# v loaded and cast to bf16 by GpSimd's own DMA queue instead of SyncE's loads and ScalarE's cast

## The chip, the core and the metric

The kernel runs on one core of one Trainium2 chip. The metric is device time in microseconds for one execution. Engines are called PE (TensorE), DVE (VectorE), ACT (ScalarE), POOL (GpSimd) and SP (SyncE, which issues DMAs). PEld is PE's weight load.

## The reference

Attention over 8 batches of 8 heads (576 rows, 64 columns a head) that keeps only the 32 largest scores of each row, and behind it two matmuls with a PReLU between them.

```python
def _attn_ref(q, k, v):
    scores = scale * np.matmul(q, k.transpose(0, 1, 3, 2))
    kth = np.partition(scores, -top_k, axis=-1)[..., -top_k:-top_k + 1]
    mask = scores >= kth
    scores = np.where(mask, scores, -1000000000.0)
    ...                                   # softmax over the kept scores
    return np.matmul(attn, v).astype(np.float32)

def _moe_ref(x, w_in, w_out, alpha):
    h = x @ w_in
    g = np.maximum(h, 0.0) + alpha * np.minimum(h, 0.0)
    return (g @ w_out).astype(np.float32)
```

The heads' outputs side by side are x, of 4608 rows and 512 columns; w_in goes to 2048 columns and w_out back to 512. All inputs and the output are float32.

## The kernel before, in words

The 64 heads are taken as 32 pairs. A pair has nine row blocks: eight of 128 rows (four per head) and a ninth that holds the last 64 rows of both heads. So there are 288 row blocks. The main loop counts ticks n, one per row block, and in each tick it writes instructions for several blocks at different stages. The order that is written is the order in which each engine's queue runs (a manual schedule). Steps that belong to a pair rather than to a row block are put into a calendar by `put(tick, eng, f)` and written by `run(tick, eng)`; "end" is the last place of a tick.

What happens to one row block, with the lines of the profile:

- PE computes scores into `ps` (L328). ACT adds a bias from `NT` (a guess at the limit of the row, made per pair from q and k) and writes `b` (L337), takes signs with a sum (`h`, L343), and the exponential `e` of two blocks at once (L348).
- POOL turns the sum of signs into a sign word `SG` (L353).
- DVE flips the scores by it (`y`, L359), takes the eight largest of six segments (`C`, L369), merges them (`L`, L384 and L386), picks one as the limit (L397 to L413), and seven blocks later compares `b` with the limit: `mk` (L433).
- POOL multiplies `mk` with `e` into the weights `w` (L443; for the ninth block `wm`, L443 and L449). SP issues the transposes of `w` into `wT` (L456, L451). PE multiplies `wT` with `v_bf` into `pu` (L494), DVE takes the reciprocal of the row sums (`rz`), and ACT scales the result into `xb` (L523).

Behind that run the two matmuls of the second part (`ph` L697, `gT` L703, `pz` L715), fed in between. Their weights are loaded in the first ticks; `w_in` comes through POOL's own DMA queue, eight loads with a cast to bf16 (L632).

In a tick, POOL's queue holds the product `w` of a block seven ticks back and then `SG` of the last block; DVE's queue holds `mk`, then the searches, then `y`. `w` needs `mk` of the same tick, and `y` needs `SG` of the same tick.

v is handled per pair. `v_bf` (six buffers) has ten column groups of 65: five of the first head, five of the second; group 4 holds only rows 0 to 63 and group 5 only rows 64 to 127, the other halves are zero. The 65th column is one, so that the matmul also gives row sums. `load_v(p)` (L147 to L154) issues four loads on SP into a float32 staging tile `st_v` (two buffers): 128 partitions x 4 rows, 64 rows, 64 rows and 128 x 4 rows, every row of 64 float32 values. `act_v` (L203) casts all of it to `v_bf` on ACT, a step of the pair's plan:

```python
ts = [-14, -13, -12, -11, -10, -9, -7, -6, -5, -5, -4, -4, -3, -2, -8]
...
dict(dve=[dve_6]), dict(act=[act_v])]
```

The last entry of `ts` places the cast eight ticks ahead of `BASE[p]`, which for the first pairs is the tick of the pair's first block (9 p). Pairs 12 and on have their plans 9 to 18 ticks earlier. The loads of `load_v` are written 13 ticks ahead of `BASE[p]`. For pair 0 the cast comes in tick -2, ahead of the first bias pass.

Of the kernel before, what the change touches and what calls it, by code (L numbers as in the profile page):

```python
# [9 lines left out]
FP32 = mybir.dt.float32  # L10
# [6 lines left out]
S = 576  # L17
# [15 lines left out]
def kernel(  # L33
# [10 lines left out]
    nc = tc.nc  # L44
    B, H, S_, D = q.shape
# [5 lines left out]
    NPAIR = (B * H) // 2  # L51
# [7 lines left out]
    V1 = D + 1  # L59
# [31 lines left out]
    vf = v.rearrange("b h s d -> (b h) s d")  # L91

    main = ExitStack()
    prep = main.enter_context(tc.tile_pool(name="prep", bufs=2))
# [13 lines left out]
    M8 = prep.tile([128, NT], FP32, name="M8", bufs=1)  # L108
    GKs = [prep.tile([128, 130], BF16, name=f"GK{i}", bufs=1) for i in range(2)]
    ksts = [prep.tile([128, 5, 130], FP32, name=f"kst{i}", bufs=1) for i in range(2)]  # L110
    st_vs = [prep.tile([128, 10, D], FP32, name=f"st_v{i}", bufs=1) for i in range(2)]
    NV = 6
    v_bfs = [prep.tile([128, 10, V1], BF16, name=f"v_bf{i}", bufs=1) for i in range(NV)]
    NQ = 5
# [2 lines left out]
    def early_sets():  # L117
        for i in range(2):
            nc.gpsimd.memset(ksts[i][:, :, 0:1], 1.0)
            nc.gpsimd.memset(ksts[i][:, :, 129:130], 1.0)  # L120
            nc.gpsimd.memset(ksts[i][64:128, 4, :], 0.0)
        for t_ in st_vs:
            nc.vector.memset(t_[64:128, 4, :], 0.0)
            nc.vector.memset(t_[0:64, 5, :], 0.0)
        for t_ in v_bfs:
            nc.vector.memset(t_[:, :, D:V1], 1.0)
            nc.vector.memset(t_[64:128, 4, D:V1], 0.0)
            nc.vector.memset(t_[0:64, 5, D:V1], 0.0)
        for i in range(KW):
            nc.vector.memset(iota[:, i:i + 1], (1.0 + 2 * i) ** 2)  # L130

    pairs = {}

    def load(p, eng2=None):
        hA = 2 * p
        st_q = prep.tile([128, 5, 128], FP32, name="st_q")
        st_k = ksts[p % 2]
        for src, st, o, en in ((qf, st_q, 0, nc.sync), (kf, st_k, 1, eng2 or nc.sync)):
            for side in range(2):
                en.dma_start(  # L140
                    st[:, 0:4, o + 64 * side:o + 64 * side + 64],
                    src[hA + side, 0:512, :].rearrange("(c p) d -> p c d", p=128))
            en.dma_start(st[0:64, 4, o:o + 128].rearrange("p (h d) -> p h d", h=2),
                         src[hA:hA + 2, 512:S, :].rearrange("h p d -> p h d"))
        pairs[p] = dict(q=st_q, k=st_k, st_v=st_vs[p % 2], v=v_bfs[p % NV])

    def load_v(p):  # L147
        hA = 2 * p
        st_v = st_vs[p % 2]
        nc.sync.dma_start(st_v[:, 0:4, :], vf[hA, 0:512, :].rearrange("(c p) d -> p c d", p=128))  # L150
        nc.sync.dma_start(st_v[0:64, 4, :], vf[hA, 512:S, :])
        nc.sync.dma_start(st_v[64:128, 5, :], vf[hA + 1, 0:64, :])
        nc.sync.dma_start(st_v[:, 6:10, :],
                          vf[hA + 1, 64:S, :].rearrange("(c p) d -> p c d", p=128))  # L154

    ORDER = [divmod(n, TPP) for n in range(N0)]
    LAST = range(P0, NPAIR)
# [5 lines left out]
    n = 0  # L163
# [7 lines left out]
    BASE = {p: TPP * (p - (p > LEAD1) - (p > LEAD2)) for p in range(NPAIR)}  # L171
# [3 lines left out]
    def prep_plan(p):  # L175
        d = pairs[p]
# [21 lines left out]

        def act_q():
            nc.scalar.copy(d["qkT"][:, 0, 0:512], d["pq"])  # L200

        def act_v():
            nc.scalar.copy(d["v"][:, :, 0:D], d["st_v"])  # L203

        def pe_k():
            d["pk"] = bank("pk", [128, 512])
# [82 lines left out]
                                    ALU.bitwise_xor, ALU.bitwise_or)  # L289

        if p == 1:
            ts = [-9, -8, -7, -6, -5, -4, -3, -2, -2, -2, -2, -2, -1, -1, 1]
        else:
            ts = [-14, -13, -12, -11, -10, -9, -7, -6, -5, -5, -4, -4, -3, -2, -8]
        dvx = "dve" if p < 2 else "dvx"
        steps = [dict(pe=[pe_q]), dict(act=[act_q], pe=[pe_k]), dict(act=[act_k], pe=[pe_t]),
                 dict(act=[act_t], pe=[pe_g]), dict(act=[act_g], pe=[pe_r]),
                 dict(dve=[dve_p]), dict(pe=[pe_s]), dict(act=[act_m]), dict(dve=[dve_2]),
                 {dvx: [dve_3]}, dict(dve=[dve_4]), {dvx: [dve_4b]}, dict(dve=[dve_5]),
                 dict(dve=[dve_6]), dict(act=[act_v])]  # L300
        if p == 0:
            ts = [-16, -15, -14, -13, -12] + [-11] * 6 + [-2]
            steps = [dict(pe=[pe_q, pe_g, pe_t]), dict(act=[act_q, act_g, act_t], pe=[pe_r, pe_k]),
                     dict(dve=[dve_p]), dict(act=[act_k], pe=[pe_s]), dict(act=[act_m])] + steps[8:]
        return list(zip(ts, steps))
# [35 lines left out]
    def act_s(n):  # L341
        h = attn.tile([128, S], BF16, name="h", bufs=1)
        nc.scalar.activation(h, tiles[n]["b"], AF.Sign, accum_out=S_all[:, n:n + 1])  # L343
# [406 lines left out]
    with tc.manual_schedule(engines={E.PE, E.Activation, E.DVE, E.Pool, E.SP}):  # L750
        cal = {}

        def put(tick, eng, f):
            cal.setdefault((tick, eng), []).append(f)

        def run(tick, eng):
            for f in cal.pop((tick, eng), ()):
                f()

        def plan(p):  # L760
            for dt, st in prep_plan(p):
                for eng, fs in st.items():
                    for f in fs:
                        put(BASE[p] + dt, eng, f)
# [55 lines left out]
        plan(0)  # L820
        plan(1)
        early_sets()
        load_v(0)
        load_v(1)
        for t in range(-16, 0):
            for eng in ("act", "pool", "pe", "dve"):
                run(t, eng)
# [7 lines left out]
        n = 0  # L835
        end = max(NT + 24, 0)
        while n < end or back or after:
            for p in range(2, NPAIR):
                if n == max(0, BASE[p] - 18):
                    load(p)  # L840
                    plan(p)
                if n == max(0, BASE[p] - 13):
                    load_v(p)
            banks[0] = 2 if n >= NT else 1 if n >= N0 + 2 else 0
            if n + 1 < NT and unit_of[n + 1][2] == 0:
                scores(n + 1)
            while after:
                after.popleft()()
            if n < NT:
                n0, m, i = unit_of[n]  # L850
                if i == 0:
                    act_b(n0)
                    if m == 2:
                        run(n, "act")
                    act_s(n)
                    if m == 1:
                        run(n, "act")
                        act_e(n0)
                else:
                    act_s(n)  # L860
                    run(n, "act")
                    act_e(n0)
            run(n, "act")
            if n >= 3 and n % 3 == 0 and n - 3 < NT:
                sel_a((n - 3) // 3)
            nb = 1 if n < N0 + 2 else 2
            credit = min(credit, 0.0) + (2.4 if n >= NT else 1.9)
            first = True
            while back and credit > 0.0 and (first or nb == 2):
                pe_f, act_f, cost, takes = back[0]  # L870
                if takes and len(after) >= nb:
                    break
                back.popleft()
                pe_f()
                if act_f:
                    after.append(act_f)
                credit -= cost
                first = False
            run(n, "pe")
            if n >= NT:  # L880
                run(n, "dve")
                run(n, "dvx")
            due = wdue.get(n, ())
            for wn in due:
                if wn < NW:
                    mask(wn)
            for f in held:
                f()
            held = []
            for wn in due:  # L890
                weights(wn, wn >= NW)
                tail_of(n, wn)
            if 0 <= n - 1 < NT:
                side_of(n - 1)
            segs = seg_ops(n - LAG_S) if 0 <= n - LAG_S < NT else []
            mn = n - LAG_M
            merges = merge_ops(mn) if 0 <= mn < NT else []
            pick = bool(merges) and mn % 3 == 2
            if pick and n >= NT:
                sel_eq(mn // 3)  # L900
            lm = n - LAG_M - 3
            for i in range(max(len(segs), len(merges), 2)):
                if i < len(segs):
                    segs[i]()
                if i < len(merges):
                    merges[i]()
            run(n, "dve")
            if 0 <= lm < NT and lm % 3 == 0:
                limit(lm // 3)
            if pick and n < NT:  # L910
                sel_eq(mn // 3)
            if 0 <= n - 1 < NT:
                flip(n - 1)
            run(n, "dvx")
            if pick:
                sel_pr(mn // 3)
                held = [lambda m=mn // 3: sel_sum(m)]
                if mn % TPP == TPP - 1:
                    put(n + 2, "dve" if mn < NT - 1 else "end", lambda g=mn // TPP: check_group(g))
                    if mn == NT - 1:  # L920
                        put(n + 2, "end", checks)
                        put(n + 3, "end", final_flag)
                        put(n + 7, "end", read_flag)
            run(n, "end")
            n += 1
# [139 lines left out]
```

## Time and profile before

| | |
|---|---|
| median of three runs | 873.0 us (871.04 to 874.72) |
| profiled execution | 873.98 us |
| its span | 872.1 us |
| DVE busy | 835.1 us |
| ACT busy | 790.3 us |
| PE busy | 721.9 us |
| POOL busy | 431.0 us |
| v cast on ACT (L203) | 32 x 0.730 us |
| w product on POOL (L443) | 282 x 1.277 us |

A row of a timeline reads: start in us, duration in us, engine, line, operation, written tile <- read tiles, shapes, count, and in brackets the idle time before it with what ended it. A row of a group gives busy time in us and mean ns of one, then the idle time just before its instructions. Instructions of DVE and ACT overlap at their ends: the next one starts before the reported end of the one ahead.

### The profile page before, as it was taken

The page shows a single profiled execution, that of the slowest core. Times are in us where ns is not written, and L with a number is a line of the kernel's source. Part 1 is how long each engine was busy: PE and PEld are TensorE (multiplying, and loading weights), DVE is VectorE, ACT ScalarE, POOL GpSimd, SP SyncE. Part 2 cuts the span into 40 slices and gives each one's busy share as a digit, 9 for nine tenths or more (in the row PEclk, how much of TensorE's full clock was granted, in tenths as well). Part 3 has the DMA queues.
Part 4 walks back from the last instruction along what each step waited for, and adds up shares of the span by engine and source line. Part 5 has one row for each costly group of instructions (what it writes and reads, how often), then busy time and mean ns, then how long its engine had stood idle before and what let it go on. Part 6 is the DMA issues. An engine that isn't in the chain of part 4 may idle for free.

```text
span 872.1 us, 20608 instructions
## 1 busy us (share of the span) xinstructions
PE 721.9 (83%) x5697; PEld 428.3 (49%) x5771; DVE 835.1 (96%) x5188; ACT 790.3 (91%) x1873; POOL 431.0 (49%) x630
## 2 busy tenths in 40 slices
PE   6776688778978789787987789977897988899996
PEld 4443444334554345444454445643455554566674
DVE  4999999999999999999999999999999999999992
ACT  6999999999999999889999999989999899979861
POOL 1455545555454555545555455554554555544530
PEclk9997779899979999989998999989999999999999
DMA  7999644644665545564576445475455543535442
GB/s 161 156 178 199 131 89 90 126 91 97 135 139 107 108 102 116 100 135 95 114 154 115 98 97 116 111 136 98 92 128 121 121 103 81 106 71 100 91 96 56
DMA packets 342619, 99.37 MB, mean 114 GB/s; under 512 B 334672, under 2 KB 334944, under 8 KB 342496
## 3 DMA queue, kind: packets, MB, share of 16 engines
q1 hardware_dynamic: 340144, 95.58, 54.4%
q0 software_dynamic: 1152, 2.10, 2.0%
q8 instruction: 47, 0.77, 0.4%
q14 instruction: 76, 0.62, 0.2%
q10 hardware_dynamic: 1200, 0.30, 0.2%
HBM read 36.71 MB, written 9.44 MB: 53 GB/s over the span
## 4 chain that ended last, share of the span: by engine, by line
DVE 62%; ACT 21%; PE 12%; DMA 2%; issue 1%; POOL 1%; SPq 0%; DVEq 0%; another core or an unknown queue 0%; ACTq 0%
DVE C L369 20%; DVE y L359 9%; DVE mk L433 9%; DVE C L386 8%; DVE L L384 7%; ACT b L337 5%; ACT h L343 5%; ACT e L348 4%; PE ps L328 4%; PE pz L715 3%; PE ph L697 2%; ACT gT L703 2%; DVE P L246 2%; ACT xb L523 2%; PE pu L494 1%
## 5 line engine op out<-in xcount | busy, mean ns | idle before, releaser
L443 POOL TENSOR_TENSOR w<-mk,e 128x576 bf16<-128x576 bf16 x250 | 319.3, 1277 | 337.9 <-DVE mk L433 187.5
L369 DVE MAX8 C<-y 128x8 f32<-128x96 f32 x1728 | 419.1, 243 | 0.1
L328 PE MATMUL ps<-qkT 64*128 64x288 f32 (+1 forms) x1280 | 256.5, 474 | 35.1 <-ACT b L337 34.6
L337 ACT ACTIVATE b<-ps,NT 128x576 f32<-128x576 f32 x288 | 202.3, 761 | 3.1 <-PE ps L328 3.1
L343 ACT ACTIVATE h<-b 128x576 bf16<-128x576 f32 x288 | 202.9, 705 | 1.7
L697 PE MATMUL ph<-xT,w_in_b 128*128 128x128 bf16 (+2 forms) x997 | 150.4, 292 | 40.8 <-ACT gT L703 33.6
L328 PEld LDWEIGHTS ps<-qkT 64*128 64x128 f32 (+1 forms) x1280 | 134.3, 194 | 97.6 <-ACT b L337 59.8
L348 ACT ACTIVATE e<-b 128x1152 bf16<-128x1152 f32 (+1 forms) x158 | 174.2, 1102 | 0.0
L384 DVE MAX8 L<-C 128x8 f32<-128x48 f32 x864 | 162.6, 188 | 0.1
L359 DVE TENSOR_SCALAR y<-b,SG 128x576 int32<-128x576 int32 x288 | 147.0, 510 | 8.2 <-POOL SG L353 7.8
L433 DVE TENSOR_SCALAR mk<-b,KP 128x576 bf16<-128x576 f32 x282 | 143.6, 509 | 0.0
L715 PE MATMUL pz<-w_out_b,gT 128*128 128x512 bf16 x543 | 132.4, 380 | 1.2 <-issue 0.5
L697 PEld LDWEIGHTS <-w_in_b 128*128 128x128 bf16 x1024 | 80.4, 100 | 104.0 <-issue 79.6
L703 ACT ACTIVATE gT<-ph 128x512 bf16<-128x512 f32 x140 | 86.0, 621 | 28.1 <-PE ph L697 28.1
L386 DVE MATCH_REPLACE8 C<-L,C 128x48 f32<-128x48 f32 x576 | 108.3, 188 | 0.0
L715 PEld LDWEIGHTS <-gT 128*128 128x128 bf16 x560 | 51.6, 98 | 68.5 <-issue 14.0
L494 PE MATMUL pu<-v_bf,wT 128*128 128x65 bf16 (+1 forms) x1600 | 69.4, 198 | 14.4 <-DMA wT<-w 6.9
L494 PEld LDWEIGHTS <-wT 128*128 128x128 bf16 (+1 forms) x1600 | 65.2, 103 | 25.6 <-issue 10.2
L353 POOL TENSOR_SCALAR SG<-S_all 128x1 int32<-128x1 f32 x288 | 65.3, 227 | 18.9 <-ACT h L343 18.8
L443 POOL TENSOR_TENSOR wm<-mk,e 128x576 bf16<-128x576 bf16 x32 | 40.8, 1276 | 49.9 <-DVE mk L433 45.6
L343 ACT ACTIVATION_READ_ACCUMULATOR h<-b 128x1 f32 x288 | 62.8, 218 | 0.0
L523 ACT ACTIVATE xb<-pu,rz 128x64 bf16<-128x64 f32 x224 | 54.5, 369 | 0.0
(113 smaller groups left out, 728.1 us busy)
## 6 DMA issues: line engine op xcount, KB each, us to landing
out_dram<-o_sb SPq DMA_DIRECT2D x34, 256.0 KB, 2.3
st_q<-in_q_dram SPq DMA_DIRECT2D x64, 128.0 KB, 2.8
st_v<-in_v_dram SPq DMA_DIRECT2D x64, 128.0 KB, 2.6
kst<-in_k_dram SPq DMA_DIRECT2D x62, 128.0 KB, 2.6
w_stage<-in_moe_w_out_dram SPq DMA_DIRECT2D x16, 256.0 KB, 3.1
w_in_b<-in_moe_w_in_dram POOLq DMA_DIRECT2D x8, 256.0 KB, 6.4
wT<-w SPq DMA_TRANSPOSE x128, 3.3
st_q<-in_q_dram SPq DMA_DIRECT2D x32, 32.0 KB, 2.5
```

Source lines behind the costliest of these rows:

```text
L328: nc.tensor.matmul(o_, l_, r_, start=True, stop=True)
L337: nc.scalar.activation(t["b"].rearrange("p (a c) -> p a c", a=2), t["ps"], AF.Identity, bias=NT0[:, p * TPP + j:p * TPP + j + 1], scale=ON ...
L343: nc.scalar.activation(h, tiles[n]["b"], AF.Sign, accum_out=S_all[:, n:n + 1])
L348: nc.scalar.activation(e, tiles[n0]["bu"], AF.Exp, scale=scl)
L359: nc.vector.tensor_scalar(t["y"].bitcast(I32), t["b"].bitcast(I32), FLIP, SG[:, n:n + 1], ALU.bitwise_xor, ALU.bitwise_xor)
L369: return [lambda g=g: nc.vector.max(out=C[:, n % TPP, g, :], in_=t["y"][:, g * SEG:(g + 1) * SEG]) for g in range(NSEG)]
L384: ops.append(lambda r=r, src=src: nc.vector.max(out=L[:, 8 * r:8 * r + 8], in_=src))
L386: ops.append(lambda r=r, src=src: nc.vector.match_replace(out=C2, in_to_replace=L[:, 8 * r:8 * r + 8], in_values=src, imm_value=NEG))
L433: nc.vector.tensor_scalar(t["mk"], t["b"], row_limit(n), None, ALU.is_ge)
L443: nc.gpsimd.tensor_tensor(dst, t["mk"], t["e"], ALU.mult)
L697: nc.tensor.matmul(hold[f][:, i, :], w_in_b[:, kk, (f + i) * 128:(f + i + 1) * 128], xT[:, kk, c0:c0 + tb], start=(kk == 0), stop=(kk == N ...
L715: nc.tensor.matmul(pz[0:m], hold["gT"][:, f, r0:r0 + m], w_out_b[:, f, :], start=False, stop=(f == NFT - 1))
```

## The change

The staging tile, its memsets, the four loads on SP and the cast on ACT go. Instead POOL issues four DMAs a pair that read float32 and write bf16 straight into `v_bf`: the two large ones first, then the two of 64 rows. Each stands at the end of one tick, in four ticks that follow each other, from nine ticks ahead of `BASE[p]` on (ticks 2 to 5 for pair 0, 7 to 10 for pair 1). There they come behind that tick's `w` and `SG` in POOL's queue. The zero halves of groups 4 and 5 are now set in `v_bf` itself, once for each of the six buffers.

```diff
-    st_vs = [prep.tile([128, 10, D], FP32, name=f"st_v{i}", bufs=1) for i in range(2)]
...
-        for t_ in st_vs:
+        for t_ in v_bfs:
+            nc.vector.memset(t_[:, :, D:V1], 1.0)
             nc.vector.memset(t_[64:128, 4, :], 0.0)
             nc.vector.memset(t_[0:64, 5, :], 0.0)
-        for t_ in v_bfs:
-            nc.vector.memset(t_[:, :, D:V1], 1.0)
-            nc.vector.memset(t_[64:128, 4, D:V1], 0.0)
-            nc.vector.memset(t_[0:64, 5, D:V1], 0.0)
...
-    def load_v(p):
-        hA = 2 * p
-        st_v = st_vs[p % 2]
-        nc.sync.dma_start(st_v[:, 0:4, :], vf[hA, 0:512, :].rearrange("(c p) d -> p c d", p=128))
-        nc.sync.dma_start(st_v[0:64, 4, :], vf[hA, 512:S, :])
-        nc.sync.dma_start(st_v[64:128, 5, :], vf[hA + 1, 0:64, :])
-        nc.sync.dma_start(st_v[:, 6:10, :],
-                          vf[hA + 1, 64:S, :].rearrange("(c p) d -> p c d", p=128))
+    def load_v(p, i):
+        hA, vb = 2 * p, v_bfs[p % NV]
+        dst, src = ((vb[:, 0:4, 0:D], vf[hA, 0:512, :].rearrange("(c p) d -> p c d", p=128)),
+                    (vb[:, 6:10, 0:D], vf[hA + 1, 64:S, :].rearrange("(c p) d -> p c d", p=128)),
+                    (vb[0:64, 4, 0:D], vf[hA, 512:S, :]),
+                    (vb[64:128, 5, 0:D], vf[hA + 1, 0:64, :]))[i]
+        nc.gpsimd.dma_start(dst, src)
...
-        def act_v():
-            nc.scalar.copy(d["v"][:, :, 0:D], d["st_v"])
...
-            ts = [-14, -13, -12, -11, -10, -9, -7, -6, -5, -5, -4, -4, -3, -2, -8]
+            ts = [-14, -13, -12, -11, -10, -9, -7, -6, -5, -5, -4, -4, -3, -2]
...
-                 dict(dve=[dve_6]), dict(act=[act_v])]
+                 dict(dve=[dve_6])]
...
-        load_v(0)
-        load_v(1)
...
+            for p in range(NPAIR):
+                i = n - (2 + 5 * p if p < 2 else BASE[p] - 9)
+                if 0 <= i < 4:
+                    put(n, "end", lambda p=p, i=i: load_v(p, i))
...
-                if n == max(0, BASE[p] - 13):
-                    load_v(p)
```

More of the change, by code (lines that the diff above doesn't have):

```diff
@@ L144, in load @@
                          src[hA:hA + 2, 512:S, :].rearrange("h p d -> p h d"))
-        pairs[p] = dict(q=st_q, k=st_k, st_v=st_vs[p % 2], v=v_bfs[p % NV])
-    def load_v(p):
-        hA = 2 * p
-        st_v = st_vs[p % 2]
-        nc.sync.dma_start(st_v[:, 0:4, :], vf[hA, 0:512, :].rearrange("(c p) d -> p c d", p=128))
-        nc.sync.dma_start(st_v[0:64, 4, :], vf[hA, 512:S, :])
-        nc.sync.dma_start(st_v[64:128, 5, :], vf[hA + 1, 0:64, :])
-        nc.sync.dma_start(st_v[:, 6:10, :],
-                          vf[hA + 1, 64:S, :].rearrange("(c p) d -> p c d", p=128))
+        pairs[p] = dict(q=st_q, k=st_k, v=v_bfs[p % NV])
+    def load_v(p, i):
[5 more added lines that the diff above has]
+        nc.gpsimd.dma_start(dst, src)
     ORDER = [divmod(n, TPP) for n in range(N0)]
@@ L291, in prep_plan @@
         if p == 1:
-            ts = [-9, -8, -7, -6, -5, -4, -3, -2, -2, -2, -2, -2, -1, -1, 1]
+            ts = [-9, -8, -7, -6, -5, -4, -3, -2, -2, -2, -2, -2, -1, -1]
         else:
-            ts = [-14, -13, -12, -11, -10, -9, -7, -6, -5, -5, -4, -4, -3, -2, -8]
+            ts = [-14, -13, -12, -11, -10, -9, -7, -6, -5, -5, -4, -4, -3, -2]
         dvx = "dve" if p < 2 else "dvx"
@@ L299, in prep_plan @@
                  {dvx: [dve_3]}, dict(dve=[dve_4]), {dvx: [dve_4b]}, dict(dve=[dve_5]),
-                 dict(dve=[dve_6]), dict(act=[act_v])]
+                 dict(dve=[dve_6])]
         if p == 0:
-            ts = [-16, -15, -14, -13, -12] + [-11] * 6 + [-2]
+            ts = [-16, -15, -14, -13, -12] + [-11] * 6
             steps = [dict(pe=[pe_q, pe_g, pe_t]), dict(act=[act_q, act_g, act_t], pe=[pe_r, pe_k]),
```

## The prediction

> **What bounds the kernel now.** I read the page's first lines first, then a table of stretches, then who waits for whom. The profiled execution took 873.98 us by the times: 872.1 us of span and 1.9 us around it.
>
> ```profile
> span 872.1 us, 20608 instructions
> ...
> PE 721.9 (83%) x5697; PEld 428.3 (49%) x5771; DVE 835.1 (96%) x5188; ACT 790.3 (91%) x1873; POOL 431.0 (49%) x630
> ```
>
> VectorE (DVE) is busy 96% of the span, ScalarE (ACT) 91%, GpSimd (POOL) 49%. Averages hide stages, so the stretches come next (columns: stretch, its length, busy time of PE, PEld, DVE, ACT, POOL, then clock, DMA share, GB/s).
>
> ```profile
> 12.00:30.00 18.00, 13.47 (x65) 8.56 (x63) 13.25 (x79) 17.58 (x36) 4.73 (x12) 1.00 0.84 173
> 30.00:75.00 45.00, 34.32 (x196) 19.77 (x198) 44.16 (x273) 44.70 (x101) 25.28 (x36) 0.96 1.08 176
> 75.00:150.00 75.00, 58.05 (x412) 33.63 (x419) 71.95 (x449) 72.52 (x174) 37.75 (x55) 0.80 0.61 122
> 150.00:750.00 600.00, 502.21 (x3966) 289.12 (x4020) 599.64 (x3742) 565.19 (x1380) 313.26 (x442) 0.95 0.55 112
> ```
>
> From 12 to 30 us ACT sets the pace (17.58 of 18.00) and DVE idles 4.75 us. From 150 to 750 us DVE works 599.64 of 600.00: nothing that ACT or SP gains there can show. The only room is DVE's idle time from 30 to 750 us: 0.84 + 3.05 + 0.36 = 4.25 us, of which the waits view names 3.9:
>
> ```profile
> DVE P L246 <- PE pr L238: 2.2, 2, 1.9
> DVE rz L511 <- PE pu L494: 1.1, 1, 1.1
> DVE sq L271 <- ACT M L267: 0.6, 1, 0.6
> ```
>
> **What is removed.** First the cast, then two of the four loads by SyncE (SP):
>
> ```profile
> L203 ACT CAST v_bf<-st_v 128x640 bf16<-128x640 f32 x32 | 23.3, 730 | 1.7 <-DMA st_v<-in_v_dram 1.7
> ```
> ```profile
> L150 SPq DMA_DIRECT2D st_v<-in_v_dram x32: 379/575/1748, 6.5 to 721.3; - x32
> L151 SPq DMA_DIRECT2D st_v<-in_v_dram x32: 497/522/629, 7.2 to 721.9; - x32
> ```
>
> ACT loses 32 x 0.73 = 23.3 us. Of these, 31 casts lie after 30 us, where DVE is the pace: worth 0, with the 4.25 us of idle time above as a ceiling. The cover is DVE's full queue, and it stays. SP loses 128 issues of some 0.55 us; its transposes of w may start sooner, which only the waits of DVE on PE (2.2 + 1.1 us) could show. I take 0.5 us of gain for both together, from 0 to 3.9.
>
> The first cast is different: it stands in front of the first bias pass.
>
> ```profile
> 11.07 0.73 ACT L203 CAST v_bf<-st_v 128x640 bf16<-128x640 f32 x1 [1.72 <-DMA st_v<-in_v_dram]
> 11.71 1.37 ACT L337 ACTIVATE b<-ps,NT 128x576 f32<-128x576 f32 x2
> ```
> ```profile
> 9.18 2.29 PE L328 MATMUL ps<-qkT 64*128 64x288 f32 x8 [0.28 <-ACT qkT L212]
> ```
> ```profile
> 10.46 0.17 DVE L288 TENSOR_SCALAR NT<-sq 128x9 int32<-128x9 int32 x1
> ```
>
> ACT waited 1.72 us for v and cast for 0.73. But b needs NT, ready at 10.63, and ps, whose eight passes end at 11.47. So what is late next is ps: b moves from 11.71 to between 10.63 and 11.47, a gain of 0.24 to 1.08. Three quarters of the passes suffice for the first row block (9.18 + 1.72 = 10.90), plus a handover of about 0.2: 11.1, gain **0.6 us**. ACT has no pause up to 24 us, so the gain carries on.
>
> The memsets of v_bf on DVE are wider now, but stand ahead of all other work, where DVE waits for the first data (busy 13.25 of 18 us even in the stretch after): 0.
>
> **What is added.** POOL issues 128 DMAs, four a pair: two of 128x4 rows and two of 64 rows, one per row block, each right behind SG of that block in POOL's order. Behind each issue in the queue wait the next product w<-mk,e and the next SG; DVE's y waits for that SG, so a late issue reaches DVE two instructions on. What v itself needs is no issue: it is read some 20 row blocks later, and three blocks take 8.4 us (y at 198.65 and at 207.02, below). How long does POOL take to issue one? The only rows are the eight weight loads:
>
> ```profile
> L632 POOL DMA_DIRECT2D w_in_b<-in_moe_w_in_dram x8: 535/591/762, 18.8 to 52.9; - x8
> ```
> ```profile
> q0 software_dynamic: 1152, 2.10, 2.0%
> ```
>
> Median 0.591 us, with 1152 / 8 = 144 packets: 128 rows and 16 more. A large v load has 512 rows, so 528 packets; a small one 80. If the time doesn't depend on packets, a large issue costs 0.59; if it is all packets, 528/144 x 0.591 = 2.17 and a small one 0.33. On SP, 128x4 rows take 0.575 us to issue and 64 rows 0.522: eight times the rows for a tenth more. That is the nearest row for the growth, though of another engine, so I take a point a third of the way up: **1.1 us** for a large issue, 0.6 for a small one. The Trainium skill's page "DMA: Bandwidth & Descriptors" (Anatomy of one DMA — SWDGE (gpsimd) path) calls descriptor generation a small cost of which much can be emitted before it grows; no run here shows that, and by it the large issue would be near 0.59.
>
> How much room is there? Here are the four places where the issues for one pair (pair 8) would stand, POOL first, then y; the other steady pairs look alike:
>
> ```profile
> 194.94 0.23 POOL L353 TENSOR_SCALAR SG<-S_all 128x1 int32<-128x1 f32 x1
> 197.15 1.27 POOL L443 TENSOR_TENSOR w<-mk,e 128x576 bf16<-128x576 bf16 x1 [1.98 <-DVE mk L433]
> 198.39 0.23 POOL L353 TENSOR_SCALAR SG<-S_all 128x1 int32<-128x1 f32 x1
> 199.74 1.27 POOL L443 TENSOR_TENSOR w<-mk,e 128x576 bf16<-128x576 bf16 x1 [1.12 <-issue]
> 200.98 0.22 POOL L353 TENSOR_SCALAR SG<-S_all 128x1 int32<-128x1 f32 x1
> 202.60 1.28 POOL L443 TENSOR_TENSOR w<-mk,e 128x576 bf16<-128x576 bf16 x1 [1.40 <-DVE mk L433]
> 203.84 0.23 POOL L353 TENSOR_SCALAR SG<-S_all 128x1 int32<-128x1 f32 x1
> 205.35 1.28 POOL L443 TENSOR_TENSOR w<-mk,e 128x576 bf16<-128x576 bf16 x1 [1.29 <-issue]
> 206.60 0.23 POOL L353 TENSOR_SCALAR SG<-S_all 128x1 int32<-128x1 f32 x1
> ```
> ```profile
> 198.65 0.52 DVE L359 TENSOR_SCALAR y<-b,SG 128x576 int32<-128x576 int32 x1
> ...
> 201.43 0.51 DVE L359 TENSOR_SCALAR y<-b,SG 128x576 int32<-128x576 int32 x1
> ...
> 204.28 0.50 DVE L359 TENSOR_SCALAR y<-b,SG 128x576 int32<-128x576 int32 x1
> ...
> 207.02 0.50 DVE L359 TENSOR_SCALAR y<-b,SG 128x576 int32<-128x576 int32 x1
> ```
>
> Room is POOL's pause behind SG, plus how long the following SG lies done before its y. Blocks in order: 1.98 + 0.03 = 2.01; 1.12 + 0.23 = 1.35; 1.40 + 0.21 = 1.61; 1.28 + 0.19 = 1.47. The first two take the large issues, the last two the small ones. So a large issue is free up to **1.35 us**, a small one up to 1.47; beyond that each pair costs the excess, as DVE has no slack to take it back. At 1.1 and 0.6 the 30 steady pairs cost 0. At 2.17 they cost 30 x (0.82 + 0.16) = 29 us. POOL's pause is thus the cover: POOL is the second engine to have hardly any.
>
> In the start the issues of pairs 1 and 2 and two weight loads meet:
>
> ```profile
> 41.22 1.27 POOL L632 DMA_DIRECT2D w_in_b<-in_moe_w_in_dram  x2
> 42.50 1.29 POOL L443 TENSOR_TENSOR w<-mk,e 128x576 bf16<-128x576 bf16 x1
> ```
>
> There the pause is already full (w starts as the second issue ends), and a small and a large v issue join: 0.6 + 1.1 = **1.7 us** later on DVE, between 0.33 + 0.59 = 0.9 and 0.59 + 2.17 = 2.8. The other v issues of the start stand where POOL waits longer for ACT or DVE; I count them at 0.
>
> The sum on the profiled execution: 873.98 - 0.6 - 0.5 + 1.7 + 0 = 874.6. The execution lay 1.0 us above the median of 873.0, so against the median: 873.6.
>
> **A rule that speaks against the change.** Two DVE instructions run while those two weight loads are issued:
>
> ```profile
> 41.32 0.52 DVE L359 TENSOR_SCALAR y<-b,SG 128x576 int32<-128x576 int32 x1
> 41.75 0.52 DVE L433 TENSOR_SCALAR mk<-b,KP 128x576 bf16<-128x576 f32 x1
> ```
> ```profile
> 18.79 1.30 POOL L632 DMA_DIRECT2D w_in_b<-in_moe_w_in_dram  x2
> ```
>
> Two issues took 1.27 us beside y and mk, and 1.30 us at 18.79, and neither y nor mk is longer than elsewhere. So I add nothing. The Trainium skill's page "SBUF — State Buffer" (Who interferes with whom) says that a DVE instruction in a two-port mode and GpSimd shut each other out of a shared port, so that descriptors cannot be written meanwhile. These rows don't show it for 144 packets; for 528 nothing does.
>
> **The rivals.**
> *The issue grows with packets, in part.* A large issue of 1.5 to 1.9 us: at 1.75 the tight block costs 0.40 a pair, 30 x 0.40 = 12 us, and the start 0.65 more: 886. For it: four times the rows; against it: SP's rows. It turns the result slower (by over 4.4 us) from 1.48 us on. Chance 0.24.
> *It grows in proportion.* 2.17 us: 29 us and 1.1 more at the start: 904. For it: nothing measured a fixed part on POOL. Chance 0.13.
> *y and mk hold an issue up.* They stand right behind SG, as the issues do; if an issue stood still for their 0.95 us (41.32 to 42.27), a large one is 2.05 and a small one 1.55: 30 x (0.70 + 0.04 + 0.08) = 25 us, 899. Against it: 1.27 beside 1.30. Chance 0.08.
> *The idle time goes.* If POOL's issues are near 0.6, and half of DVE's 8.6 us of idle time from 12 to 150 us was due to ACT's and SP's work: 873.0 - 4.3 - 1.1 + 0.9 = 868.5. Against it: the largest named wait is on PE. Chance 0.09.
> That the loads stay on SP or the cast on ACT can be left out: the changed program has neither, and 128 loads more on POOL.
>
> **How the numbers follow.** The forecast, issues that fit, has 0.46: 873.6, by itself from 870 to 877.4, the latter at 1.48 us. A difference under 0.5%, 4.4 us, is about what a measurement of this kernel can tell from no change. Faster is the last rival: 0.09. Within: 0.46. Slower: 0.24 + 0.13 + 0.08 = 0.45. The range goes from 868 to 900: it takes in the held-up issues and leaves out the proportional case and a little at the low end, 0.16 in all.
>
> **What would show it.** The group of v's DMA on POOL has 128 instructions; the mean of the large ones decides: under 1.35 us means no wait of y on SG after the start, over 1.5 means some hundred such waits and DVE's busy share in 150 to 750 us below 99%. ACT's busy time should fall by 23 us and DVE's stay at 835. The first b should start near 11.1. I am wrong if the time leaves 870 to 877 with large issues under 1.35 us, or if y and mk get longer than 0.52 us.

## The result, and the profile after

| | before | after |
|---|---|---|
| median of 15 runs each | 874.39 us (871.04 to 879.07) | 879.81 us (877.66 to 884.60) |
| ratio, 95% interval | | 1.0061 (1.0042 to 1.0081) |
| profiled execution, span | 873.98, 872.1 | 879.81, 878.0 |

The change costs 0.61%, 5.4 us. With 15 runs the median of before is 874.4 instead of the 873.0 of three. The forecast's own case ended at 877.4, so its upper side was left; the range, 868 to 900, was not.

The busy line of the page, answering to the one the prediction began with:

```profile
span 878.0 us, 20651 instructions
PE 738.2 (84%) x5771; PEld 433.4 (49%) x5771; DVE 842.0 (96%) x5184; ACT 771.2 (88%) x1841; POOL 526.6 (60%) x758
```

POOL has 95.6 us more and ACT 19.1 us less, as intended. The line that matters is DVE: 842.0 instead of 835.1, although it has four instructions fewer. Its idle time is 36.0 us instead of 37.0. So the 5.9 us of span are 6.9 us more work on DVE, less 1.0 us of idle time. In sum DVE waits no longer than before; instructions got longer. The table of stretches (same columns as before) says the same:

```profile
12.00:30.00 18.00, 11.42 (x65) 7.41 (x64) 13.27 (x80) 17.59 (x36) 7.36 (x16) 0.72 0.80 129
30.00:75.00 45.00, 35.31 (x198) 20.48 (x198) 42.75 (x261) 42.60 (x97) 32.63 (x47) 0.62 1.15 175
150.00:750.00 600.00, 512.30 (x3953) 292.28 (x3950) 599.37 (x3707) 544.37 (x1340) 386.33 (x540) 0.93 0.64 105
```

From 150 to 750 us DVE is as full as before (599.37 and 599.64) and gets less done: 3707 instructions instead of 3742. Its idle time grows by 0.27 us there and from 30 to 75 us, from 0.84 to 2.25; in the other stretches it is the same or less.

Which instructions got longer? The groups of DVE by form, before and then after (busy, mean ns | idle before):

```profile
L359 DVE TENSOR_SCALAR y<-b,SG 128x576 int32<-128x576 int32 x288 | 147.0, 510 | 8.2 <-POOL SG L353 7.8
L433 DVE TENSOR_SCALAR mk<-b,KP 128x576 bf16<-128x576 f32 x282 | 143.6, 509 | 0.0
```
```profile
L361 DVE MAX8 C<-y 128x8 f32<-128x96 f32 x1728 | 418.8, 243 | 0.1
L351 DVE TENSOR_SCALAR y<-b,SG 128x576 int32<-128x576 int32 x288 | 149.4, 519 | 8.6 <-POOL SG L345 8.3
L425 DVE TENSOR_SCALAR mk<-b,KP 128x576 bf16<-128x576 f32 x282 | 148.0, 525 | 0.0
```

y gained 2.4 us and mk 4.4 us: 6.8 together, all but 0.1 us of DVE's increase. MAX8, the largest group, has 243 ns in both kernels. And the issues themselves (group; then the tile's row with min/median/max; then the queue):

```profile
L149 POOL DMA_DIRECT2D v_bf<-in_v_dram x128 | 101.8, 795 | 0.6 <-issue 0.3
```
```profile
L149 POOL DMA_DIRECT2D v_bf<-in_v_dram x128: 559/837/992, 15.0 to 752.9; - x128
```
```profile
q0 software_dynamic: 40064, 6.82, 10.3%
```

The longest of 128 issues took 0.99 us, so all are below the free 1.35. The packets are as counted: 64 x (528 + 80) + 1152 = 40064.

Now the four ticks of one pair. First POOL's issues, then DVE's y and mk in the same ticks (timeline):

```profile
196.48 0.84 POOL L149 DMA_DIRECT2D v_bf<-in_v_dram  x1
199.97 0.92 POOL L149 DMA_DIRECT2D v_bf<-in_v_dram  x1
202.72 0.60 POOL L149 DMA_DIRECT2D v_bf<-in_v_dram  x1
205.66 0.87 POOL L149 DMA_DIRECT2D v_bf<-in_v_dram  x1
```
```profile
197.50 0.52 DVE L351 TENSOR_SCALAR y<-b,SG 128x576 int32<-128x576 int32 x1
197.93 0.52 DVE L425 TENSOR_SCALAR mk<-b,KP 128x576 bf16<-128x576 f32 x1
...
200.06 0.52 DVE L351 TENSOR_SCALAR y<-b,SG 128x576 int32<-128x576 int32 x1
200.49 0.66 DVE L425 TENSOR_SCALAR mk<-b,KP 128x576 bf16<-128x576 f32 x1
...
202.99 0.59 DVE L351 TENSOR_SCALAR y<-b,SG 128x576 int32<-128x576 int32 x1
...
205.91 0.50 DVE L351 TENSOR_SCALAR y<-b,SG 128x576 int32<-128x576 int32 x1
```

The first issue is over before y starts: nothing happens. The second is still running when mk starts: mk takes 0.66 us, 0.15 more than its mean before. y, which starts 0.09 us behind the same issue, is not longer. The third runs when y starts, 0.27 us behind it: y takes 0.59, 0.08 more. The fourth, of 64 rows like the third, took 0.87 instead of 0.60: y had started at 205.91, 0.25 us behind the issue's start, and here the issue was held up and y (0.50) was not. Such a pair costs DVE 0.15 + 0.08 = 0.23 us. Most pairs look like this one, not all: in the whole trace mk is longer in 29 ticks and y in 26, and the two groups' 6.8 us are the sum to go by.

### The profile page after: what moved, and what is told of

Read it like the earlier page. It is cut to its first block, busy times and chain, and to the rows that moved or that the text cites. A ratio compares the mean times of both kernels' runs of the same rounds, so it can differ in the third digit from the quotient of the medians.

```text
span 878.0 us, 20651 instructions
## 1 busy us (share of the span) xinstructions
PE 738.2 (84%) x5771; PEld 433.4 (49%) x5771; DVE 842.0 (96%) x5184; ACT 771.2 (88%) x1841; POOL 526.6 (60%) x758
## 3 DMA queue, kind: packets, MB, share of 16 engines
q0 software_dynamic: 40064, 6.82, 10.3%
## 4 chain that ended last, share of the span: by engine, by line
DVE 67%; ACT 15%; PE 13%; DMA 2%; POOL 1%; issue 1%; SPq 0%; DVEq 0%
DVE C L361 22%; DVE y L351 10%; DVE mk L425 10%; DVE C L378 8%; DVE L L376 8%; PE ps L320 4%; ACT b L329 4%; PE pz L707 3%; ACT h L335 3%; ACT e L340 3%; DVE P L238 2%; PE ph L689 2%; ACT gT L695 2%; ACT xb L515 1%; DVE L L395 1%; DVE KK L399 1%
## 5 line engine op out<-in xcount | busy, mean ns | idle before, releaser
L320 PE MATMUL ps<-qkT 64*128 64x288 f32 (+1 forms) x1280 | 262.8, 485 | 32.4 <-ACT b L329 32.1
L689 PE MATMUL ph<-xT,w_in_b 128*128 128x128 bf16 (+2 forms) x1024 | 156.3, 299 | 40.1 <-ACT gT L695 27.0
L320 PEld LDWEIGHTS ps<-qkT 64*128 64x128 f32 (+1 forms) x1280 | 138.8, 200 | 94.9 <-ACT b L329 57.1
L351 DVE TENSOR_SCALAR y<-b,SG 128x576 int32<-128x576 int32 x288 | 149.4, 519 | 8.6 <-POOL SG L345 8.3
L425 DVE TENSOR_SCALAR mk<-b,KP 128x576 bf16<-128x576 f32 x282 | 148.0, 525 | 0.0
L707 PE MATMUL pz<-w_out_b,gT 128*128 128x512 bf16 x560 | 135.1, 380 | 0.0
L149 POOL DMA_DIRECT2D v_bf<-in_v_dram x128 | 101.8, 795 | 0.6 <-issue 0.3
```

The source lines that it names most:

```text
L320: nc.tensor.matmul(o_, l_, r_, start=True, stop=True)
L351: nc.vector.tensor_scalar(t["y"].bitcast(I32), t["b"].bitcast(I32), FLIP, SG[:, n:n + 1], ALU.bitwise_xor, ALU.bitwise_xor)
L425: nc.vector.tensor_scalar(t["mk"], t["b"], row_limit(n), None, ALU.is_ge)
L689: nc.tensor.matmul(hold[f][:, i, :], w_in_b[:, kk, (f + i) * 128:(f + i + 1) * 128], xT[:, kk, c0:c0 + tb], start=(kk == 0), stop=(kk == N ...
L707: nc.tensor.matmul(pz[0:m], hold["gT"][:, f, r0:r0 + m], w_out_b[:, f, :], start=False, stop=(f == NFT - 1))
```

## The experiments

The theory: POOL's issue and DVE's y and mk exclude each other while they overlap, and the price is y and mk getting longer. Rivals: the removals cost something themselves; the cast inside the DMA is the cause; the transfers themselves, wherever they are issued; the POOL queue's delay. Where a kernel loads v only in part or not at all, `v_bf` is set to ones throughout beforehand; that adds 3.2 us to DVE's busy time in the first 12 us, where it waits for data (7.26 us without v, 4.06 in the changed kernel). Ratios are to the kernel before on the same chip, whose median lay between 874.27 and 874.61. The recorded times of DVE's groups drift from one profile to the next by up to some 5 ns an instruction (MAX8 from 241 to 247 ns), so y and mk are compared with each other as well.

**The removals alone.**

```diff
-            for p in range(NPAIR):
-                i = n - (2 + 5 * p if p < 2 else BASE[p] - 9)
-                if 0 <= i < 4:
-                    put(n, "end", lambda p=p, i=i: load_v(p, i))
```

> The changed kernel without any load of v: no issue on GpSimd, no load on SyncE, no cast on ScalarE (the value buffers stay at one, so the output leaves v out). It shows what the removals are worth alone. Theory (VectorE is the pace, the removals buy next to nothing, and the whole loss comes from GpSimd's issues): 0 to 2 us below the kernel before, VectorE busy at 835 us, mk at 509 ns and y at 510 ns. Rival (the loss comes from what was removed, for instance from ScalarE running ahead and disturbing the order): 878 to 880 us here too.

Measured: 873.41 us, ratio 0.9987 (0.9971 to 1.0003). y and mk are equal again:

```profile
L351 DVE TENSOR_SCALAR y<-b,SG 128x576 int32<-128x576 int32 x288 | 148.0, 514 | 7.4 <-POOL SG L345 7.0
L425 DVE TENSOR_SCALAR mk<-b,KP 128x576 bf16<-128x576 f32 x282 | 144.6, 513 | 0.0
```

The removals are worth 1.1 us (2.5 to -0.3 by the interval), as the sum had it; the loss is in what is added, some 6.5 us. PE's granted clock, lower behind the change than before it from 12 to 75 us (0.72 and 0.62 instead of 1.00 and 0.96), is as low in this kernel (0.69 and 0.67), which is not slower; so it is not the cause.

**Two of the four issues.** The first and the fourth, and in another kernel the second and the third.

```diff
-                if 0 <= i < 4:
+                if i in (0, 3):
```
```diff
-                if 0 <= i < 4:
+                if i in (1, 2):
```

> The changed kernel with only the first (128x4 rows) and the fourth (64 rows) of the four issues of a pair (the other half of v is left out). Theory (a GpSimd issue costs VectorE time only where its descriptors are written while y or mk wants its two ports; by the trace that is the mk behind the second issue, +0.15 us, and the y behind the third, +0.08 us): mk and y as before the change, VectorE busy near 835 us, the time at most 1 us from the kernel with no load at all. Rival (each issue costs the same, 128 share 5.4 us): half of the loss, 2.7 us above that kernel.

> The changed kernel with only the second (128x4 rows) and the third (64 rows) issue of a pair (the other half of v is left out). Theory of the ports: nearly the whole loss stays: mk +0.15 us and y +0.08 us once a pair, VectorE busy near 842 us, 6 to 7 us above the kernel with no load. Rival (each issue costs the same): 2.7 us above it.

Measured: 874.67 (1.0003, 0.9984 to 1.0023) and 879.79 (1.0057, 1.0038 to 1.0077). The groups of the first of these kernels, then of the second:

```profile
L351 DVE TENSOR_SCALAR y<-b,SG 128x576 int32<-128x576 int32 x288 | 149.3, 519 | 7.9 <-POOL SG L345 7.3
L425 DVE TENSOR_SCALAR mk<-b,KP 128x576 bf16<-128x576 f32 x282 | 144.3, 512 | 0.0
```
```profile
L351 DVE TENSOR_SCALAR y<-b,SG 128x576 int32<-128x576 int32 x288 | 149.8, 520 | 8.0 <-POOL SG L345 7.5
L425 DVE TENSOR_SCALAR mk<-b,KP 128x576 bf16<-128x576 f32 x282 | 148.8, 527 | 0.0
```

The second and third issue alone cost as much as all four. In the kernel with the first and fourth, y has 519 against mk's 512: the fourth issue now does lengthen y. Its rows in one pair (POOL, then DVE):

```profile
202.33 0.59 POOL L149 DMA_DIRECT2D v_bf<-in_v_dram  x1
```
```profile
202.60 0.57 DVE L351 TENSOR_SCALAR y<-b,SG 128x576 int32<-128x576 int32 x1
```

y starts 0.27 us behind the issue and is the one held up. In the changed kernel it was 0.25 us, and the issue was. So it is not the place in the code that decides but some 0.02 us of order. The border is not the same to the hundredth everywhere: beside the third issue of the kernel with two, y is the longer one from 0.25 us on.

**Loads without a cast.** POOL loads float32 into the staging tile at the same four places, and ACT casts as before, six ticks later in most pairs.

```diff
-        nc.sync.dma_start(st_v[:, 0:4, :], vf[hA, 0:512, :].rearrange("(c p) d -> p c d", p=128))
...
+        nc.gpsimd.dma_start(dst, src)
...
-            ts = [-14, -13, -12, -11, -10, -9, -7, -6, -5, -5, -4, -4, -3, -2, -8]
+            ts = [-14, -13, -12, -11, -10, -9, -7, -6, -5, -5, -4, -4, -3, -2, -2]
```

> The kernel before with v's four loads issued by GpSimd at the same four places as in the change, but still as float32 into the staging tile, with ScalarE's cast kept (moved some ticks later, so that it does not wait). Theory of the ports: the issue, not the cast in the DMA, is what costs: VectorE busy near 842 us, 5 to 7 us above the kernel before, as with the change. Rival (the conversion on the way makes the issue or the transfer dear): mk and y as before and the time within 1 us of the kernel before.

Measured: 893.36, 1.022 (1.019 to 1.025). The time is no answer, since DVE now also waits for PE behind the moved cast. Its waits (us in total, times, longest), and the groups:

```profile
DVE P L246 <- PE pr L238: 10.4, 8, 1.9
```
```profile
L359 DVE TENSOR_SCALAR y<-b,SG 128x576 int32<-128x576 int32 x288 | 149.3, 519 | 9.2 <-POOL SG L353 9.0
L433 DVE TENSOR_SCALAR mk<-b,KP 128x576 bf16<-128x576 f32 x282 | 148.4, 526 | 0.0
L154 POOL DMA_DIRECT2D st_v<-in_v_dram x128 | 101.1, 790 | 0.2 <-issue 0.2
```

The durations are an answer: issues of 790 ns against 795 with the cast, y and mk of 519 and 526 against 519 and 525. The cast in the DMA makes neither dearer. The queue's line shows one thing more:

```profile
q0 software_dynamic: 6272, 11.54, 5.8%
```

The same rows are far fewer packets here, 6272 instead of 40064, and an issue takes as long. So what its time goes with is rows and not packets.

The same with the cast three ticks later in most pairs. Here the next pair's rows overwrite the staging tile before the cast in two pairs, so that those hold the wrong v; the work is the same.

```diff
-            ts = [-14, -13, -12, -11, -10, -9, -7, -6, -5, -5, -4, -4, -3, -2, -2]
+            ts = [-14, -13, -12, -11, -10, -9, -7, -6, -5, -5, -4, -4, -3, -2, 1]
```

> The earlier kernel with float32 loads by GpSimd into the staging tile, with ScalarE's cast ten ticks after the first of them instead of seven, so at a place of the nine-tick cycle where the kernel before has it. Theory: the 19 us of the earlier one were two things, 6 us of stretched y and mk as in the change and the rest ScalarE's cast at a bad place (VectorE's P waited 10.4 us for PE); here 5 to 8 us above the kernel before, mk at 525 ns. Rival (float32 transfers through GpSimd's queue are dear by themselves): 15 us or more again.

Measured: 887.4, 1.0135 (1.0109 to 1.0162), again above what was expected. y and mk are the same (519, 525), but POOL's issues waited 8.7 us and y 14.5 us for SG. How much of these two kernels' time is the cast's place stays open.

**The issue ahead of SG.** There it runs beside DVE's searches (MAX8 and the like) instead of y and mk, and SG stands behind it.

```diff
-                    put(n, "end", lambda p=p, i=i: load_v(p, i))
+                    put(n, "presg", lambda p=p, i=i: load_v(p, i))
...
+            run(n, "presg")
             side_of(n - 1)
```

> The changed kernel with each issue of v moved one place ahead in GpSimd's queue: behind the product w and ahead of SG in the same tick, so that it runs beside VectorE's searches and not beside y and mk. Theory of the ports: y and mk return to 510 to 514 ns although all 128 issues and their transfers stay. But SG comes an issue later, and y has room of 0.95, 0.03, 0.23 and 0.21 us in the four ticks: waits of 0 + 0.81 + 0.37 + 0.39 us a pair (issues of 0.84, 0.84, 0.60, 0.60 us), some 48 us more waiting of y for SG, 915 to 925 us in all. Rival (the transfers or the mere number of issues stretch y and mk, not what runs beside them): y and mk stay at 519 and 525 ns.

Measured: 924.81, 1.0579 (1.0557 to 1.0600). A wait of DVE, and its groups:

```profile
DVE y L351 <- POOL SG L345: 55.7, 98, 2.9
```
```profile
L351 DVE TENSOR_SCALAR y<-b,SG 128x576 int32<-128x576 int32 x288 | 148.5, 515 | 56.0 <-POOL SG L345 55.7
L425 DVE TENSOR_SCALAR mk<-b,KP 128x576 bf16<-128x576 f32 x282 | 144.5, 512 | 0.0
```

Nearly all of the loss is now a wait for SG, 55.7 us instead of 7.8, in 98 ticks; y and mk are back at the level of the kernel without v. DVE's busy time is as high as in the changed kernel (842.2), but not because an instruction got longer: where DVE waits, the overlap of one instruction with the next is gone. So 128 issues beside the searches, with all their transfers, lengthen nothing, and it takes the overlap with y or mk. This kernel also shows what the room was worth that the prediction counted: without it the same issues cost 50 us.

**The size.** Only the second issue of a pair, once with half its rows (256) and once with 1152.

```diff
-                    (vb[:, 6:10, 0:D], vf[hA + 1, 64:S, :].rearrange("(c p) d -> p c d", p=128)),
+                    (vb[:, 6:8, 0:D], vf[hA + 1, 64:320, :].rearrange("(c p) d -> p c d", p=128)),
...
-                if 0 <= i < 4:
+                if i == 1:
```
```diff
+                    (vb[:, 0:9, 0:D], vr[2 * S * p:2 * S * p + 2 * S, :].rearrange("(c p) d -> p c d", p=128)),
```

> Only the second issue of each pair, at its place, with half the rows (128x2, 256 rows; the rest of v is left out). Theory with a price by descriptors: mk waits for the writing of the descriptors, 0.15 us at 528 packets, so about 0.08 us at 272: mk's group 2.3 us above the kernel with no load, and the time as much. Rival (a fixed price of handing the port over): 0.15 us again, 4.2 us.

> Only the second issue of each pair, at its place, with 128x9 rows (1152 rows in one issue; they land in other column groups than the matmul expects, so the output leaves v out). By 528 packets in 0.84 us and 80 in 0.60 us the issue takes about 1.2 us, still inside the room of 1.35 us. Price by descriptors: mk 0.33 us longer in that tick, 9 to 10 us above the kernel with no load. Rival (fixed price): 0.15 us, 4 to 5 us above it.

Measured: 874.45 (1.0010, 0.9994 to 1.0027) and 883.44 (1.0103, 1.0085 to 1.0120). Issue and mk of one tick, with 256 rows and then with 1152:

```profile
198.21 0.79 POOL L149 DMA_DIRECT2D v_bf<-in_v_dram  x1
```
```profile
198.74 0.52 DVE L425 TENSOR_SCALAR mk<-b,KP 128x576 bf16<-128x576 f32 x1
```
```profile
198.99 1.20 POOL L151 DMA_DIRECT2D v_bf<-in_v_dram  x1
```
```profile
199.52 0.93 DVE L427 TENSOR_SCALAR mk<-b,KP 128x576 bf16<-128x576 f32 x1
```

The half issue leaves mk as it is, where I had expected 0.08 us a tick (the time doesn't decide it: 2.0 us above the kernel without v by the ratios, with intervals that overlap); the large one costs 0.42 where I had expected 0.33. The price is not in proportion to rows. One rule fits: where mk or y starts more than some 0.25 us behind the issue's start, it is longer by (end of the issue - its own start - 0.25 us), if that is above zero. With 256 rows 199.00 - 198.74 = 0.26: 0.01. With 512, in the changed kernel, 200.89 - 200.49 = 0.40: 0.15. With 1152, 200.19 - 199.52 = 0.67: 0.42. For y beside the third issue, 203.32 - 202.99 = 0.33: 0.08; beside the fourth of the kernel with two issues, 202.92 - 202.60 = 0.32: 0.07. It is not only these ticks: in the changed kernel, from 60 us on, 85 y and mk start that far behind an issue, and all of them follow the rule within 0.02 us, as do the 29 mk of either kernel here. A y that starts earlier behind the issue is first, and the rule doesn't hold for it: 0.09 us behind the second issue y takes 0.52, and the issue 0.92 instead of 0.84.

**The small issues four ticks later.**

```diff
-                if 0 <= i < 4:
+                if i in (0, 1, 6, 7):
...
+                    (vb[64:128, 5, 0:D], vf[hA + 1, 0:64, :]))[i if i < 2 else i - 4]
```

> The changed kernel, all of v loaded, with the two small issues of a pair moved from its third and fourth tick to its seventh and eighth, where y starts 0.03 us behind SG (in the third and fourth: 0.2 us), so y has the port before GpSimd asks for it. Theory (who comes first keeps the port): y back to 510 to 514 ns, mk unchanged at 525 ns: 2 to 3 us below the changed kernel. Rival (any issue beside y and mk costs): no gain, or the price moves to mk.

Measured: 878.43, 1.0045 (1.0028 to 1.0062).

```profile
L351 DVE TENSOR_SCALAR y<-b,SG 128x576 int32<-128x576 int32 x288 | 146.9, 510 | 8.5 <-POOL SG L345 7.9
L425 DVE TENSOR_SCALAR mk<-b,KP 128x576 bf16<-128x576 f32 x282 | 147.6, 524 | 0.0
```

y is at 510 ns again and mk at 524, so y's part is gone and mk's stays. Against the kernel before, the loss is 4.2 us instead of 5.4; the intervals overlap, so the durations show this and the time does not.

**Five issues.** The second large one in two halves, the first of them at its place and the second in the seventh tick, the small ones in the eighth and ninth.

```diff
-                    (vb[:, 6:10, 0:D], vf[hA + 1, 64:S, :].rearrange("(c p) d -> p c d", p=128)),
+                    (vb[:, 6:8, 0:D], vf[hA + 1, 64:320, :].rearrange("(c p) d -> p c d", p=128)),
+                    (vb[:, 8:10, 0:D], vf[hA + 1, 320:S, :].rearrange("(c p) d -> p c d", p=128)),
...
-                if 0 <= i < 4:
+                if i in (0, 1, 6, 7, 8):
```

> The changed kernel, all of v loaded, with the second large issue cut into two of 128x2 rows and all but the first issue of a pair moved to ticks where y starts 0.03 to 0.14 us behind SG: five issues a pair, in its first, second, seventh, eighth and ninth tick. Theory (a DVE instruction that starts ahead of GpSimd's writing keeps the port, and mk is stretched only by what the issue lasts beyond 0.25 us after mk's start, which for 272 and 80 packets is nothing): y and mk at 509 to 514 ns, and with more issues than the changed kernel the time falls by 5 us to that of the kernel with no load, 872 to 875 us, within 0.3% of the kernel before. Rival (each issue has its price): 160 issues cost more than 128, 880 us or above.

Measured: 876.59, 1.0028 (1.0012 to 1.0045). The groups:

```profile
L352 DVE TENSOR_SCALAR y<-b,SG 128x576 int32<-128x576 int32 x288 | 147.4, 512 | 8.6 <-POOL SG L346 8.0
L426 DVE TENSOR_SCALAR mk<-b,KP 128x576 bf16<-128x576 f32 x282 | 144.7, 513 | 0.0
L150 POOL DMA_DIRECT2D v_bf<-in_v_dram x160 | 124.6, 779 | 0.8 <-issue 0.5
```

With a quarter more issues and 23 us more of them on POOL, the kernel is faster than with four: y and mk are at 512 and 513 ns, as without any v load (514 and 513), and DVE's busy time is 838.8 us instead of 842.0. Of the loss of 5.4 us, 3.4 are gone. The median lies 1.6 us above the expected stretch. Of the 2 us that are left against before, the trace names a part. mk and y still have 1.1 and 0.4 us more than before. And the pile-up of the start, told below, is in this kernel too, in another form (POOL, then DVE):

```profile
44.16 1.32 POOL L436 TENSOR_TENSOR w<-mk,e 128x576 bf16<-128x576 bf16 x1
```
```profile
44.26 1.32 DVE L390 TENSOR_TENSOR EQ<-ra,iota 128x72 f32<-128x72 f32 x1
45.70 0.52 DVE L352 TENSOR_SCALAR y<-b,SG 128x576 int32<-128x576 int32 x1
```

y starts at 45.70 us as in the changed kernel (45.75), but here DVE doesn't stand idle before it: one EQ takes 1.32 us instead of 0.2, for as long as POOL's product runs beside it. That these parts are the whole rest is not shown. No version here beats the kernel before, and the kernel without v puts what this order of work could gain at 1.1 us.

## Why the prediction was right, and where it was wrong

The time lay in the range and on the slower side. The forecast case, though, fell by the sentence it named: y and mk got longer than 0.52 us while every issue stayed under 1.35. That the range held is luck for the most part: it reached to 900 for rivals that did not come true, and none of them priced what happened.

*The length of an issue* held. The large ones take 0.84 us alone (estimate 1.1) and the small ones 0.60 (estimate 0.6). Neither bound was right: with 64, 512 and 1152 rows, 0.60, 0.84 and 1.20 us (the last one with y 0.10 us behind its start, so perhaps held up a little), so some 0.57 us and 0.55 ns a row, a rise far from proportional. The prediction counted packets; the loads without a cast showed that rows are the measure. The rivals of growth in part (1.5 to 1.9 us) and in proportion (2.17 us) are out.

*The room in POOL's queue* held too: y's waits for SG are 8.3 us in 6 times, against 7.8 in 6.

```profile
DVE y L351 <- POOL SG L345: 8.3, 6, 3.3
```

*"So I add nothing"* is the step that failed. I had put the question whether POOL's issues and DVE exclude each other to one pair of rows: two issues of 128 rows that took 1.27 us beside y and mk and 1.30 elsewhere. Both sums hide what the single issues show. At 41.22 us the first took 0.73, with y 0.10 us behind its start, and the second 0.53; at 18.79, with neither y nor mk beside them, the first took 0.76 for another reason, which stays open, and the second 0.54. The trace before has a cleaner pair at 25.07 us: 0.58 alone, and 0.71 with y 0.08 us behind its start. So POOL's issues were held up in the kernel before already. That y and mk were not longer there is the order again: y was first, the first issue ended 0.20 us into mk, within the 0.25 us that cost nothing, and the second began when mk was already running. The rival that I gave 0.08 had the exclusion but the wrong side: it let POOL stand still for 0.95 us and priced POOL's lateness at 25 us. In the runs POOL loses at most 0.27 us, inside its room, and DVE loses 0.15 in most of the 29 ticks of mk, where there is no room at all. The price is 6.8 us, and not 25.

The Trainium skill's page "SBUF — State Buffer" (Who interferes with whom) says that the ports which DVE shares with GpSimd are locked exclusively, that whoever issues first keeps them, and that a DVE instruction with at most one input from SBUF and outside the two-port modes does not take part. The runs agree on order (0.25 us against 0.27 us decides which side is late) and on the searches (no price beside 128 issues). They add a size: a DVE instruction is not held for the whole issue but for what is left of it past 0.25 us. The runs show that issue and instruction exclude each other; that a port is what they share, no run shows.

*The first bias pass* was to gain 0.6. The rows of ACT and PE after:

```profile
11.83 1.37 ACT L329 ACTIVATE b<-ps,NT 128x576 f32<-128x576 f32 x2 [2.15 <-PE ps L320]
```
```profile
9.51 2.29 PE L320 MATMUL ps<-qkT 64*128 64x288 f32 x8 [0.28 <-ACT qkT L204]
```

As predicted, ps is what is late next. But b waited for all eight passes (9.51 + 2.29 = 11.80) and not for three quarters of them, the lower of the two bounds, 0.24; and PE started 0.33 us later than before, so that b came 0.12 later instead of earlier. That start differs from one profile to the next, from 9.16 to 9.51 us in the kernels here. In the kernel without v the same eight passes took 1.24 us, and b, which then waited for NT, started at 10.88: there the gain was had. Why the passes take 2.29 us in most profiles and 1.24 in three was not tried.

*The pile-up at the start* was put at 1.7 us. POOL, then DVE:

```profile
41.58 1.48 POOL L149 DMA_DIRECT2D v_bf<-in_v_dram  x2
43.05 1.10 POOL L624 DMA_DIRECT2D w_in_b<-in_moe_w_in_dram  x2
44.14 1.38 POOL L435 TENSOR_TENSOR w<-mk,e 128x576 bf16<-128x576 bf16 x1
45.50 0.21 POOL L345 TENSOR_SCALAR SG<-S_all 128x1 int32<-128x1 f32 x1
```
```profile
45.75 0.52 DVE L351 TENSOR_SCALAR y<-b,SG 128x576 int32<-128x576 int32 x1 [1.36 <-POOL SG L345]
```

It is there, at the predicted place and in the predicted form, with 1.36 us. The 1.4 us that DVE is idle longer from 30 to 75 us are this wait.

*ACT's relief* hid as said: 599.37 of 600 us on DVE. ACT's busy time fell by 19.1 and not 23; in the timeline before, b started 0.09 us ahead of the cast's reported end, and 32 such overlaps, counted once in busy time, are 2.9 of the 4.2 missing.

The terms by measurement: -1.1 from the kernel with the removals alone, +1.4 for the pile-up, +6.8 for y and mk: 7.1, where the medians differ by 5.4 and the profiled spans by 5.9. The excess of some 1 us is within what these intervals can tell; the stretches also have 1.3 us less idle time on DVE from 75 to 150 us (1.71 instead of 3.05), which none of the terms holds.

## What to carry to other kernels

When work goes to an engine that has room, ask not only whether it fits there but which instructions of the bounding engine will run beside it, and look whether their mean duration moves: a busy time that grows with no new wait is the sign. If the bounding engine has some instructions that a DMA issue of GpSimd disturbs and others that it doesn't, short issues that end before the first kind starts, or soon after, cost that engine nothing, and splitting one in two can be cheaper than leaving it whole. A test of such a disturbance must have the size and the order in time that are to be used, and must look at both sides: here an issue of a quarter of the rows seemed to show none, because y came first and the issue, not y, was longer.

## What the runs showed of the hardware that I had not expected

- POOL's issue and DVE's two tensor-scalar instructions hold each other up, and 0.02 us of order decides which one is longer: y 0.25 us behind the issue's start left y at 0.50 and the issue at 0.87 instead of 0.60; 0.27 us behind it left the issue at 0.59 or 0.60 and y at 0.57 to 0.59.
- The price for DVE has a threshold. An issue that began more than 0.25 us ahead of mk and ends 0.26 us into it costs 0.01, one that ends 0.40 into it 0.15, one that ends 0.67 into it 0.42.
- An issue with a cast from float32 to bf16 takes as long as one without: 795 and 790 ns in the mean, though the queue has 40064 packets in the one case and 6272 in the other.
- EQ, a DVE tensor-tensor instruction of 0.2 us, gets longer beside POOL's product w: it took 1.32 us with five issues, 0.67 with the small issues later and 0.69 with the half issue, and ended 0.1 us behind the product each time.
- From one profile to the next the recorded times of DVE's groups drift together by a few ns an instruction, whatever its length (from the kernel before to the one without v, MAX8 243 to 247 ns, the one of 48 elements 188 to 193, mk 509 to 513), so a group is better compared with another group of the same profile than with the same group of another.
